# Real and imaginary parts of 64 states in one tile, two more folds of cells and one scan: one core, a gated mix of a state-space layer and linear attention

## The chip, the cores and the metric

The kernel runs on one core of one Trainium2 chip. The metric is device time in microseconds (us) of a whole execution. A core has TensorE (PE in the profile; its weight loads are PEld), VectorE (DVE), ScalarE (ACT), GpSimd (POOL) and SyncE (SP). SP, ACT and POOL also issue DMA transfers.

## The reference

Two branches read the same input x (2048 × 512) and are mixed by a gate per token. Branch A is a diagonal state-space layer with 512 complex states; branch B is linear attention with 32 heads of width 16, whose feature map is a pair of softmaxes.

```python
def _A_ref(x, ...):
    dt = exp(log_dt); Lam_bar = exp(dt * Lam)
    B_bar = ((Lam_bar - 1.0) / Lam)[:, None] * Bmat
    Bu = einsum("bld,pd->blp", x, B_bar)
    for t in range(L):
        h = Lam_bar * h + Bu[:, t, :]
    return 2.0 * einsum("blp,dp->bld", hseq, Cmat).real + x * Dskip

def _B_ref(x, wqkv, w_phi, wo):
    # q, k, v of 32 heads; pq = q @ w_phi, pk = k @ w_phi
    phi_q = concat([softmax(pq), softmax(-pq)]); phi_k = concat([softmax(pk), softmax(-pk)])
    kv = phi_k^T v; z = sum(phi_k)
    return ((phi_q kv) / (phi_q z + 1e-6)) @ wo

g = sigmoid((x * gate_w).sum(-1))
return g * a + (1 - g) * b
```

## The kernel before

**The recurrence by cells.** The 2048 time steps are 256 cells of 8; position r of a cell is the remainder r. States come in four tiles of 128 (index j), real and imaginary parts in separate planes. `b` (line 607 on) projects x on B for the even positions into `eb`; `g` projects an odd position, adds the even one before it times lambda, and goes on folding (lambda², lambda⁴), all as matmuls with diagonal matrices `dg`; a complex product of two planes is two matmuls for each plane. After three doublings `vv[j]` holds what a whole cell of 8 adds. `z` (line 658 on) runs the scan over the 256 cells on VectorE: it rotates by tabulated angles (`T2c`, `T2s`, made by `i`), scans real and imaginary parts with the real decay r⁸, and rotates back. Then the other positions of each cell are restored from the scan: `H` (position 3), `h` (1 and 5) and `p` (0, 4, 2, 6), each a complex multiple of an earlier state added to what `b` or `g` left.

In `h` and `p` this is done in two ways. For j < 2, ScalarE or VectorE scales (`scaled`, lines 434 to 438) into a scratch tile and a DMA issued by POOL adds it to its target in SBUF (`add_by_dma`, line 647). For j ≥ 2 VectorE adds.

**The output.** `y` multiplies the states of 128 tokens with C (`C2`, scaled by `c`), `o` is the attention numerator and denominator, `O` transposes its result by DMA, `t` multiplies with wo on top of `y` in the same PSUM bank and takes it out with the gate, `R` stores. Output tiles come in the order of `ORD = (7, 3, 5, 1, 0, 4, 2, 6)`, two tiles of tokens for each remainder: y0 and y1 need only the scan, y2 and y3 `H`, y4 to y7 `h`, y8 to y15 `p`.

**Branch B.** `k`, `v`, `q` are projections, their PSUM taken out to `Xq` and `vx`; `x`, `n`, `e`, `s` (`X`, `N`, `E`, `S` for Q) are maximum, minimum, exponentials and sums of the features; `a` accumulates keys times values, and in spare columns the gate's dot product, as 64 one-column matmuls. `S` ends in two DMA transposes into `phT`.

**What sets the order.** Every engine and every DMA queue runs its instructions in the order of one written list, `ORDER` (lines 24 to 52). A token is the next step of a stage: `g011@6` is a step of `g` for tile 0, second odd position, imaginary part, in PSUM bank 6; `:D` puts an eviction or scaling on VectorE in place of ScalarE. The order within one engine is the list's; across engines only data and buffers hold a step back.

Of the kernel before, what the change touches and what calls it, by code (L numbers as in the profile page):

```python
# [20 lines left out]
P = 128  # L21
# [27 lines left out]
S3 S3 y8 o10 p31 t8 o11@6 O3 t9 S3 S3 t6 o11 o11 p21 p31 t8 t9 y12@1 t7 p31:D y14@0 t6 t7 o11 o12@6 o12 p21 O5 p21
o13@2 u11 p31 y14 o12 o12 o13 y12 o13 R2 o14@6 o13 O6 o14 o14 o14 R4 u10 O7 y13@2 y13 o15@6 o15 o15 o15 t10 t10 R3 t11  # L50
t13 t11 u12 O8 u13 t12 t12 t13 u14 R5 t14 t14 R6 y15@54 y15 y15 t15 t15:D t15 R7 t15 R8 R8
# [5 lines left out]
KO = tuple(range(16))  # L57
XLOADS = ((2, 2), (4, 2), (6, 2), (8, 2), (10, 2), (12, 2), (14, 2))
# [12 lines left out]
def kernel(  # L71
# [24 lines left out]
    PT = Pst // P  # L96
    NTI = S // P
# [42 lines left out]
    vec_n = const.tile([12, P], BF16, name="vec_n")  # L140
# [5 lines left out]
    C2 = const.tile([P, 2, PT, D], BF16, name="C2")  # L146
    warm = const.tile([P, D], BF16, name="warm")
    nc.vector.memset(warm[:], 0.0)
    nc.scalar.dma_start(out=Wc[:], in_=B_w_phi.rearrange("(k hl) e f -> (hl e) k f", hl=8))
    wk_nat, xn = C2[:, 0], C2[:, 1]  # L150
# [4 lines left out]
    for n, src in enumerate((A_Lambda_im, A_Lambda_re, A_log_dt)):  # L155
        nc.gpsimd.dma_start(out=vec_n[4 * n:4 * n + 4, :], in_=src.rearrange("(j p) -> j p", p=P))
# [3 lines left out]
    Wq2 = const.tile([P, KT, DF], BF16, name="Wq2")  # L160
    maskN = const.tile([P, 4, 4], F32, name="maskN")
    eps_p = const.tile([P, 1], F32, name="eps_p")
    vec = const.tile([P, 5, KT], F32, name="vec")
    gw_b = const.tile([P, KT], BF16, name="gw_b")
# [5 lines left out]
    eb01 = const.tile([P, 2, 2, 2, N2], BF16, name="eb01")  # L170
    Dd = const.tile([P, KT, P], BF16, name="Dd")
    Drow = const.tile([P, D], BF16, name="Drow")
    NVX = 8
# [4 lines left out]
    H3 = pR.tile([P, PT, 2, ZP + N2 + 2], BF16, name="H3")  # L178
    H1 = pR.tile([P, PT, 2, N2], BF16, name="H1")
    Xq = pR.tile([P, NTI, D], BF16, name="Xq")  # L180
    nc.vector.memset(H3[:, :, :, 0:ZP], 0.0)
# [4 lines left out]
    dg = pBC.tile([P, 9, PT, P], BF16, name="dg")  # L186
    DG_NLI, DG_LR, DG_LI, DG_NMI, DG_MR, DG_MI, DG_NNI, DG_NR, DG_NI = range(9)
    (S_NLI, S_LR, S_LI, S_NMI, S_MR, S_MI, S_NNI, S_NR, S_NI, S_NBI, S_BR, S_NBR) = range(12)
    par = pBC.tile([P, 25, PT], F32, name="ssm_par")
    dgs = pBC.tile([P, 12, PT], F32, name="dgs")  # L190
    dgv = pBC.tile([P, 9, PT, 4], BF16, name="dgv")
    Bn = pBC.tile([P, PT, 2, D], BF16, name="Bn")
    CT = pBC.tile([P, PT, 2, D], BF16, name="CT")
    eb = [eb01[:, 0], eb01[:, 1], Bn[:, 0:2], Bn[:, 2:4]]
# [8 lines left out]
    BT = pAC.tile([P, 2, KT, Pst], BF16, name="BT")  # L203
    T2c = pAC.tile([P, PT, NC], BF16, name="T2c")
    T2s = pAC.tile([P, PT, NC], BF16, name="T2s")
    vv = [pAC.tile([P, 2, N2], BF16, name=f"vv{j}") for j in range(PT)]
# [20 lines left out]
    def st_Lb():  # L227
        for ri, src in enumerate((A_B_re, A_B_im)):
            for h in range(2):
                trans(out=BT[:, ri, 2 * h:2 * h + 2, :], in_=src[:, 2 * h * P:2 * (h + 1) * P])  # L230
                yield
# [6 lines left out]
    def st_Lc():  # L238
        for h in range(2):
            for ri, src in enumerate((A_C_re, A_C_im)):  # L240
                trans(out=CT[:, 2 * h:2 * h + 2, ri, :], in_=src[:, 2 * h * P:2 * (h + 1) * P])
                yield
# [22 lines left out]
    tab_g = tc.tile_pool(name="tabtmp", bufs=2, reuse_waits="tile")  # L265
    tabp = tab_g.__enter__()
    iot = tabp.tile([P, NC], F32, name="iot", bufs=1)
    identf = stg.tile([P, P], F32, name="identf", bufs=1)
    make_identity(nc, identf[:])
    nc.gpsimd.iota(iot[:], pattern=[[1, NC]], base=0, channel_multiplier=0, allow_small_or_imprecise_dtypes=True)  # L270
# [10 lines left out]
    lam, ldt, dsk = vec[:, 0:2, :], vec[:, 2, :], vec[:, 3, :]  # L281
# [6 lines left out]
    dt_, r_, om_, t0, t1, t2, den_, r2_, r4_, om8, r8_ = (par[:, 10 + k, :] for k in range(11))  # L288
# [30 lines left out]
    def st_V():  # L319
        pvt = bank([P, 12], BF16, "pvt")  # L320
        nc.tensor.transpose(pvt[:], vec_n[:], ident[0:12, 0:12])
        yield
        nc.vector.tensor_copy(out=vec[:, 0:3, :].rearrange("p n j -> p (n j)"), in_=pvt[:])
        yield

    def st_V2():
        pvt = bank([P, 8], BF16, "pvt")
        nc.tensor.transpose(pvt[:], vec_m[:], ident[0:8, 0:8])
        yield
        nc.vector.tensor_copy(out=vec[:, 3:5, :].rearrange("p n j -> p (n j)"), in_=pvt[:])  # L330
# [14 lines left out]
    def st_P():  # L345
        aexp(out=dt_, in_=ldt, func=ACT.Exp)
        yield
        VT(out=tha, in0=lam, in1=dt_.unsqueeze(1).to_broadcast([P, 2, KT]), op=ALU.mult)
# [12 lines left out]
    def st_P2():  # L361
        VS(out=om_, in0=th_, scalar1=INV_2PI, scalar2=None, op0=ALU.mult)
        yield
        VS(out=t0, in0=om_, scalar1=MAGIC, scalar2=MAGIC, op0=ALU.add, op1=ALU.subtract)
        yield
        VT(out=t1, in0=om_, in1=t0, op=ALU.subtract)
# [14 lines left out]
    def st_P4():  # L381
        VS(out=om8, in0=t0, scalar1=8.0, scalar2=None, op0=ALU.mult)
        yield
        VS(out=t2, in0=om8, scalar1=MAGIC, scalar2=MAGIC, op0=ALU.add, op1=ALU.subtract)
        yield
        VT(out=om8, in0=om8, in1=t2, op=ALU.subtract)
        yield

    def st_gw():
        nc.vector.tensor_copy(out=gw_b[:], in_=vec[:, 4, :])  # L390
        yield

    def square(out_r, out_i, b, t):
# [561 lines left out]
```

## Time and profile before

| | |
|---|---|
| runs (us) | 151.61, 151.03, 151.01; median 151.03 |
| span of the profiled execution | 149.4 us, 2839 instructions; its median of runs lies 1.6 us above it |
| TensorE busy | 142.8 us, 96% |
| VectorE busy | 139.0 us, 93% |
| ScalarE busy | 125.1 us, 84% |
| POOL busy | 26.6 us, 18% |
| DMA | 20.14 MB, mean 135 GB/s; SP's queue 53.1% of the engines' time, POOL's 18.6% |

A row of the page or of the groups by line reads: line, engine, operation, output <- input by the program's names, shape, count | busy us, mean ns of one | idle time of the engine before it and who ended it. The mean is the length of one instruction; neighbours overlap, so the pace of a series is shorter and is read from start times. A row of a stretch reads: from:to, length, then for TensorE, its weight loads, VectorE, ScalarE and POOL the busy us and the number of instructions, then the granted TensorE clock, the share of the 16 DMA engines and the GB/s that they moved. A share can stand a little over 1, since packets overlap. In slices each digit is the busy tenths of one of 40 equal parts of the span, 3.7 us each.

### The profile page before, as it was taken

What the parts mean: (1) busy time and instruction counts of PE and PEld (TensorE: products, weight loads), DVE (VectorE), ACT (ScalarE), POOL (GpSimd) and SP (SyncE); (2) the same over time, 40 slices, a digit from 0 to 9 for tenths busy, and PEclk for the clock granted to TensorE, in tenths of its full rate; (3) what the DMA queues carried; (4) which work ended last, traced back from release to release, by engine and by line L of the source; (5) the groups of instructions that cost most, each with busy time, mean ns of one, the idle gap of its engine ahead of it and who ended that gap; (6) DMA issues with size and microseconds to landing.
All of it is one profiled execution on the core that took longest, in us unless ns stands there. A gap on an engine that the chain in (4) does not pass through costs nothing.

```text
span 149.4 us, 2839 instructions
## 1 busy us (share of the span) xinstructions
PE 142.8 (96%) x1010; PEld 73.8 (49%) x1010; DVE 139.0 (93%) x338; ACT 125.1 (84%) x222; POOL 26.6 (18%) x42
## 2 busy tenths in 40 slices
PE   6999999999999999999999999999999999999980
PEld 2844444545545444464444467555444554455450
DVE  2899999999999999999999999999999999986880
ACT  3479999999999999999999999999989996552000
POOL 7403700000000341022605236011004200000000
PEclk9999999999999999999999999999999999999999
DMA  4999999991220174008274999908999996998742
GB/s 118 222 235 174 142 202 176 246 189 33 54 91 0 26 114 77 0 0 140 38 107 70 166 175 183 210 7 133 103 238 218 184 186 77 227 207 197 209 148 71
DMA packets 52959, 20.14 MB, mean 135 GB/s; under 512 B 44496, under 2 KB 52432, under 8 KB 52944
## 3 DMA queue, kind: packets, MB, share of 16 engines
q1 hardware_dynamic: 48000, 15.44, 53.1%
q0 software_dynamic: 4000, 4.20, 18.6%
q10 hardware_dynamic: 944, 0.31, 0.8%
q8 instruction: 8, 0.13, 0.4%
q14 instruction: 7, 0.06, 0.1%
HBM read 2.91 MB, written 2.10 MB: 33 GB/s over the span
## 4 chain that ended last, share of the span: by engine, by line
ACT 67%; PE 24%; issue 3%; DVE 2%
ACT EE L554 15%; PE PS L816 11%; ACT Xq L129 9%; PE PS L875 7%; ACT CT L436 6%; ACT vx L129 5%; ACT dg L436 4%; ACT H L129 3%; ACT vv L129 3%; ACT eb L129 3%; ACT Bn L129 3%; PE PS L316 2%; PE PS L835 2%; ACT lg L562 2%; ACT m L436 1%
## 5 line engine op out<-in xcount | busy, mean ns | idle before, releaser
L554 ACT ACTIVATE EE<-EE 128x2048 bf16<-128x2048 bf16 x16 | 32.5, 2066 | 0.2 <-DVE EE L548 0.2
L483 PE MATMUL PS<-WKV,xT 128*128 128x480 bf16 (+1 forms) x128 | 29.3, 373 | 0.2 <-DMA xT<-in_A_x_dram 0.2
L483 PEld LDWEIGHTS <-xT 128*128 128x128 bf16 x192 | 18.1, 98 | 19.4 <-DMA xT<-in_A_x_dram 0.7
L129 ACT CAST Xq<-PS 128x480 bf16<-128x480 f32 x32 | 20.1, 735 | 0.5 <-PE PS L483 0.5
L625 PE MATMUL PS<-xT,BT 128*128 128x512 bf16 x64 | 15.9, 379 | 0.0
L816 PE MATMUL PS<-C,H 128*128 128x512 bf16 x64 | 15.4, 378 | 0.5 <-DVE on L848 0.2
L875 PE MATMUL PS<-Wo,oT 128*128 128x512 bf16 (+2 forms) x68 | 15.5, 367 | 0.0
L613 PE MATMUL PS<-xT,BT 128*128 128x512 bf16 x64 | 15.4, 379 | 0.0
L483 PE MATMUL PS<-Wq,xT 128*128 128x480 bf16 x64 | 15.1, 366 | 0.0
L848 DVE TENSOR_TENSOR on<-PS,rd 128x512 bf16<-128x512 f32 x16 | 10.7, 681 | 2.3 <-ACT rd L842 2.3
L881 ACT ACTIVATE ot<-PS,G 128x512 bf16<-128x512 f32 (+1 forms) x8 | 4.9, 639 | 9.1 <-PE PS L875 9.1
L436 ACT ACTIVATE CT<-H,dgs 128x1024 bf16<-128x1024 bf16 x9 | 12.1, 1349 | 0.0
L129 ACT CAST vx<-PS 128x512 bf16<-128x512 f32 x16 | 11.7, 793 | 0.0
L648 POOL DMA_DIRECT2D C<-CT x4 | 5.4, 1352 | 35.0 <-ACT rc L566 31.8
L531 DVE TENSOR_TENSOR sm<-EE 128x2048 bf16<-128x2048 bf16 (+1 forms) x9 | 10.0, 1108 | 0.1
L542 DVE TENSOR_TENSOR EE<-Xq,mx 128x2048 bf16<-128x2048 bf16 (+1 forms) x9 | 10.0, 1109 | 0.0
L548 DVE TENSOR_TENSOR EE<-mn,Xq 128x2048 bf16<-128x2048 bf16 (+1 forms) x9 | 10.0, 1107 | 0.0
L613 PEld LDWEIGHTS <-BT 128*128 128x128 bf16 x64 | 6.3, 98 | 7.2 <-issue 0.2
L569 DVE TENSOR_TENSOR EE<-EE,rc 128x2048 bf16<-128x2048 bf16 x8 | 9.8, 1234 | 0.0
L625 PEld LDWEIGHTS <-BT 128*128 128x128 bf16 x64 | 6.1, 98 | 7.0
L875 PEld LDWEIGHTS <-oT 128*128 128x128 bf16 x68 | 6.1, 98 | 6.5 <-DMA oT<-on 0.5
L531 DVE TENSOR_TENSOR sm<-sm 128x512 bf16<-128x512 bf16 (+2 forms) x18 | 9.3, 516 | 0.0
(185 smaller groups left out, 325.8 us busy)
## 6 DMA issues: line engine op xcount, KB each, us to landing
out_dram<-ot SPq DMA_DIRECT2D x7, 256.0 KB, 2.4
C<-CT POOLq DMA_DIRECT2D x4, 256.0 KB, 3.9
eb<-CT POOLq DMA_DIRECT2D x4, 256.0 KB, 4.9
eb<-dg POOLq DMA_DIRECT2D x4, 256.0 KB, 5.9
WKV<-in_A_x_dram SPq DMA_DIRECT2D x3, 256.0 KB, 3.1
WKV<-in_B_wqkv_dram SPq DMA_DIRECT2D x1, 512.0 KB, 5.6
Wo<-in_B_wo_dram SPq DMA_DIRECT2D x1, 512.0 KB, 4.8
H<-CT POOLq DMA_DIRECT2D x2, 256.0 KB, 3.3
```

Source lines behind the costliest of these rows:

```text
L129: nc.scalar.copy(out=out_ap, in_=in_ap)
L436: nc.scalar.mul(out=out_ap, in_=in_ap, mul=s_)
L483: MM(out=pt[:], lhsT=xT[:, kt, ti * P:(ti + 1) * P], rhs=W[:, kt, :], start=(kt == 0), stop=(kt == KT - 1))
L531: VT(out=dst, in0=cur[:, :, :, 0:n, :], in1=cur[:, :, :, n:2 * n, :], op=op)
L542: VT(out=half(EE, 0), in0=X5, in1=live["mx", p].to_broadcast([P, L, 8, Dh, 4]), op=ALU.subtract)
L548: VT(out=half(live["EE", p], 1), in0=live["mn", p].to_broadcast([P, L, 8, Dh, 4]), in1=X5, op=ALU.subtract)
L554: aexp(out=EE[:, l_:l_ + 2], in_=EE[:, l_:l_ + 2], func=ACT.Exp)
L613: MM(out=pb[:], lhsT=BT[:, ri, kt, j * P:(j + 1) * P], rhs=cells(kt, 2 * pr), start=(kt == 0), stop=(kt == KT - 1))
L625: MM(out=pgq[:], lhsT=BT[:, ri, kt, js], rhs=cells(kt, r1), start=(kt == 0), stop=False)
L816: MM(out=py[:], lhsT=hs[j][ri], rhs=C2[:, 1 - ri, j, c:c + w], start=(j == 0 and ri == 0), stop=False)
L848: VT(out=live["on", g_][:, u], in0=pn[:, :, :, 0:Dh], in1=rd[:].unsqueeze(3).to_broadcast([P, 2, 16, Dh]), op=ALU.mult)
L875: MM(out=py[:], lhsT=oT[:, g, :], rhs=Wo[:, g, c:c + w], start=False, stop=(g == HG - 1))
```

## The change

- **The tiles.** Eight tiles m of 64 states take the place of four of 128: partitions 0 to 63 hold the real parts and 64 to 127 the imaginary parts. `LS[:, m, 0..2]` holds the positions that `eb` and `H1` held, `HH` what `H3` held. A complex product is now one matmul with a matrix of two diagonals (`dg[k, m]`: the real part on the diagonal, the imaginary part 64 off it). B is loaded plainly in this layout and then transposed from SBUF; C is scaled in the old layout and copied over by four transfers (`C`), and four adding transfers (`A`) put in the second term.
- **Two more folds.** `g` goes on within the 256 cells: pairs (lambda⁸) and fours (lambda¹⁶) by matmuls of 128 and 64 columns on strided columns, with an eviction between each. The scan is over 64 groups of four cells, all eight tiles side by side in one instruction of 512 columns, with a decay tile that is zero where a new tile begins. The swap of real and imaginary parts that the rotation needs is a matmul with `Sw`. `sa`, `sb` and `H` then unfold with matmuls and one VectorE addition out of PSUM each.
- **Restoring the other positions.** `UNITS` lists it: `hd0` to `hd3`, `ed0` to `ed3`, `dd0`, `dd1` take two tiles each by `by_dma`: scale the state, add by DMA, scale the half-swapped state, add by DMA. `dp4` to `dp7` take one tile each by `by_pe`: one matmul and one VectorE addition. The half-swapped states come from SP's transfers `XX0`, `XX1` (four) and `XX2` (two), which copy partitions 0 to 63 to 64 to 127 and back.
- **The gate** is column 481 of Q's weights; `q` has a third step that takes that column out of PSUM, and `G` runs four times for four tiles.
- **Buffers**: seven `vx` tiles for eight; `phT` alternates between `phT0` and one more buffer.
- **The list** is written anew.

```diff
+UNITS = ((1, 'hd0', 1), (1, 'hd1', 1), (1, 'hd2', 1), (1, 'hd3', 1), (0, 'ed0', 0), (0, 'ed1', 0), (0, 'ed2', 0), (0, 'ed3', 0), (2, 'dd0', 0), (2, 'dd1', 0), (2, 'dp4', 0), (2, 'dp5', 0), (2, 'dp6', 0), (2, 'dp7', 0))
...
+    def st_g(m, dst):
+        pg = bank([P, N2], F32, "pg")
+        bx(pg, m, (1, 3)[dst])
+        yield
+        MM(out=pg[:], lhsT=dg[:, 0, m, :], rhs=LS[:, m, 2 * dst], start=False, stop=(dst == 0), skip_group_check=True)
...
+        MM(out=pg[:], lhsT=dg[:, 1, m, :], rhs=LS[:, m, 1], start=False, stop=False, skip_group_check=True)
+        yield
+        evac(hc(m, 0, 1, NC, 1), pg[:, 0:NC])
+        yield
+        MM(out=pg[:, NC:N2], lhsT=dg[:, 2, m, :], rhs=hc(m, 0, 1, NC, 1), start=False, stop=False, skip_group_check=True)
+        yield
+        evac(hc(m, 0, 2, NC // 2), pg[:, NC:N2:2])
+        yield
+        MM(out=pg[:, NC + 1:N2:2], lhsT=dg[:, 3, m, :], rhs=hc(m, 0, 2, NC // 2), start=False, stop=False, skip_group_check=True)
+        yield
+        evac(hc(m, 1, 4, NC // 4), pg[:, NC + 1:N2:4])
+        yield
+        MM(out=pg[:, NC + 3:N2:4], lhsT=dg[:, 4, m, :], rhs=hc(m, 1, 4, NC // 4), start=False, stop=True, skip_group_check=True)
+        yield
+        evac(V2[:, m], pg[:, NC + 3:N2:4])
...
+    def st_X(q):
+        for h in range(2):
+            nc.sync.dma_start(out=HHs[h * HS:(h + 1) * HS, :, q * NC:(q + 1) * NC],
+                              in_=HH[(1 - h) * HS:(2 - h) * HS, :, ZP - 1 + q * (NC + 1):ZP - 1 + q * (NC + 1) + NC])
+            yield
+    def st_X2():
+        for h in range(2):
+            nc.sync.dma_start(out=HHs[h * HS:(h + 1) * HS], in_=LS[(1 - h) * HS:(2 - h) * HS, :, 1, :])
+            yield
+    def by_dma(i, u, k):
+        plain = prevs if u < 2 else (lambda m: pair(LS[:, m, 1]))
+        for part, (src, sc_) in enumerate(((plain, dgs[:, k, 0, :]), (lambda m: pair(HHs[:, m]), nsn[:, k, :]))):
+            t = slot(2 * (i % 2) + part)
+            for e in range(2):
+                m = 2 * i + e
+                scaled(pair(t[:, e]), src(m), sc_[:, m:m + 1])
+                yield
+            add_by_dma(LS[:, 2 * i:2 * i + 2, u], t)
+            yield
+    def by_pe(m, u, k):
+        pd = bank([P, N2], F32, "pd")
+        MM(out=pd[:], lhsT=dg[:, k, m, :], rhs=prevs(m) if u < 2 else LS[:, m, 1], start=True, stop=True)
+        yield
+        addto(LS[:, m, u], pd[:])
+        yield
...
-            for kt in range(KT):
-                MM(out=live["acc"][1][:, 4 * KVW + ti:4 * KVW + ti + 1], lhsT=xT[:, kt, ti * P:(ti + 1) * P],
-                   rhs=gw_b[:, kt:kt + 1], start=False, stop=(n_ == NTI - 1 and kt == KT - 1), skip_group_check=True)
...
+        VS(out=nge[:, n:n + 1], in0=pq[:, DF:DF + 1], scalar1=-Z_MAX, scalar2=-1.0, op0=ALU.max, op1=ALU.mult)
```

The new list from the scan to the last additions (in part):

```
G0 g71 g31 v11@6 g71 s3 g61 g31 g71 g51:D S0 g51 g31:D g51 q10@5 A v11 S0 z0@4 z0 v9 q10 v10@6 v12@7 v14@1 z0 z0 z0
...
H2@5 sb0 v13 q13 a4 a4 a4 H2 E1 q13 H0@4 Y H1@5 A H0 E1 Y S0 q11 q8@1 q11 H1 q8 XX0 Y H3@4 Ld H3 q9@2 Y S1 q9 q14@5
...
S1 N2 hd3 hd2 y3 G2 S1 hd3 t0 q12 S1 N3 O1 E2 q12 t1 E2 hd3:D q15 hd3:D y3 t0 y6@2 ed1 y2 t1 S1 hd2 hd2:D t3 t2 S1
hd2:D N3 X3 ed1:D hd3 t2 y5@5 S2 o4@6 o4 t3 S2 o4 S1 y7@3 S2 o5@0 Ld R0 y4@4 ed0:D hd2 ed1 o5 ed0:D o5 y4 S2 y4 o4
...
ed3:D t6 o8 y9@6 E3 o9 XX2 dd0:D dd1:D dd0 o10@0 o10 S3 o10 XX2 o10 t6 y11@7 y10@5 ed3 dd1 o11@0 S3 o11 y10 dp4@2
...
t10 G3 R2 S3 dd1 t8 dp7 o12@0 o13@3 o12 o13 u9 dp4 dd1 o13 t9 u10 R3 o12 y14@2 o12 y12@6 y14 o13 y12 t10 G3 u11
```

More of the change, by code (lines that the diff above doesn't have):

```diff
@@ L202 @@
     Wd = pAC.tile([P, HG, Dh - 1], BF16, name="Wd")
[L203 to L206, printed above, removed]
+    BT = pAC.tile([P, MT, KT, P], BF16, name="BT")
+    T2c = pAC.tile([P, MT, NC // 4], BF16, name="T2c")
+    T2s = pAC.tile([P, MT, NC // 4], BF16, name="T2s")
+    decay = pAC.tile([P, MT, NC // 4], F32, name="decay")
     stg_g = tc.tile_pool(name="stage", bufs=2)
@@ new lines, in st_A, with st_z @@
+    def st_A():
+        for q, pq_ in ((0, 0), (1, 1), (0, 1), (1, 0)):
+            add_by_dma(C2[q * HS:(q + 1) * HS, pq_::2], CT[pq_ * HS:(pq_ + 1) * HS, 1 - q])
+            yield
+    def st_z(b):
+        sw = pools["sw"][1]
+        n = MT // ZB
+        m0, m1 = b * n, (b + 1) * n
+        w_ = n * NC // 4
+        tc_, ts_ = T2c[:, m0:m1].rearrange("p m c -> p (m c)"), T2s[:, m0:m1].rearrange("p m c -> p (m c)")
+        v_ = V2[:, m0:m1].rearrange("p m c -> p (m c)")
+        pv = bank([P, w_], F32, "pz_")
+        MM(out=pv[:], lhsT=Sw[:], rhs=v_, start=True, stop=True)
+        yield
+        mc = sw.tile([P, w_], BF16, name="mc")
+        VT(out=mc[:], in0=v_, in1=tc_, op=ALU.mult)
@@ new lines, in st_H, with prevs, pair @@
+    def st_H(b):
+        pd = bank([P, 2, NC], F32, "pd")
+        for k in range(2):
+            MM(out=pd[:, k], lhsT=dg[:, 2, 2 * b + k, :], rhs=hc(2 * b + k, -1, 1, NC), start=(k == 0), stop=True, skip_group_check=True)
+        yield
+        addto(HH[:, 2 * b:2 * b + 2, ZP + NC:ZP + N2], pd[:])
+        yield
+    def prevs(m):
+        return HH[:, m, ZP - 1:ZP - 1 + 2 * (NC + 1)].rearrange("p (q c) -> p q c", c=NC + 1)[:, :, 0:NC]
+    def pair(t):
+        return t.rearrange("p (q c) -> p q c", c=NC)
@@ L841, in st_o @@
         rd = op_.tile([P, 2, 16], F32, name="rd")
[L842 removed]
+        aexp(out=rd[:], in_=ld[:], func=ACT.Exp, scale=-1.0, bias=nge[:, n:n + 1])
         yield
```

491 lines of the change are left out of this document (220 added, 271 removed).

## The prediction

> **What bounds the kernel now.** I read the page's busy line and slices first, then TensorE in order of time, then the DMA share by stretches, because the page shows three engines full at once.
>
> ```profile
> PE 142.8 (96%) x1010; PEld 73.8 (49%) x1010; DVE 139.0 (93%) x338; ACT 125.1 (84%) x222; POOL 26.6 (18%) x42
> PE   6999999999999999999999999999999999999980
> POOL 7403700000000341022605236011004200000000
> DMA  4999999991220174008274999908999996998742
> q1 hardware_dynamic: 48000, 15.44, 53.1%
> q0 software_dynamic: 4000, 4.20, 18.6%
> ```
>
> TensorE is busy in every slice but the first and the last two. "Busy" could still hide waits, so I look at the pace, in the timeline of TensorE, with VectorE's first read of the small PSUM tile and its last instruction (start, length, instruction):
>
> ```profile
> 8.63 0.17 DVE L323 CAST vec<-PS 128x12 f32<-128x12 bf16 x1
> ...
> 36.80 0.42 PE L599 MATMUL PS<-vx,EE 128*128 128x68 bf16 x8
> 37.05 0.24 PE L603 MATMUL PS<-gw_b,xT 128*128 128x1 bf16 x4
> 37.15 0.41 PE L599 MATMUL PS<-vx,EE 128*128 128x68 bf16 x8
> ...
> 38.37 0.27 PE L641 MATMUL PS<-vv,dg 128*128 128x256 bf16 x1
> 38.48 0.27 PE L642 MATMUL PS<-vv,dg 128*128 128x256 bf16 x1
> ...
> 41.33 1.89 PE L613 MATMUL PS<-xT,BT 128*128 128x512 bf16 x8
> 43.05 1.03 PE L625 MATMUL PS<-xT,BT 128*128 128x512 bf16 x4
> ...
> 92.36 1.89 PE L816 MATMUL PS<-C,H 128*128 128x512 bf16 x8
> ...
> 142.19 1.04 PE L816 MATMUL PS<-C,eb 128*128 128x384 bf16 x8
> 144.25 0.94 PE L875 MATMUL PS<-Wo,oT 128*128 128x384 bf16 x6
> 145.11 0.62 DVE L883 TENSOR_SCALAR ot<-PS,G 128x384 bf16<-128x384 f32 x1 [0.30 <-PE PS L875]
> ```
>
> Start to start, eight 512-column matmuls take 1.72 us, 0.215 each; a 256-column one 0.11; eight of 68 columns 0.25; the four gate columns 0.10. With these prices I added up TensorE's work along the ORDER list: 139.0 us in all, 88.3 ahead of y1 and 136.2 ahead of y15. The trace starts y1 at 92.36 and y15 at 142.19, so the list plus 4.1 (growing to 6.0) is the clock: TensorE stands still for hardly 2 us between them and is the bound. From the last tile's eviction at 145.1 to the end of the span it is another 4.3 us. The median of the three runs, 151.03, is 1.6 us over the profiled span of 149.4; I make the sum against the span and add 1.6.
>
> The third resource is the DMA, in stretches (the last two columns are the share of the 16 DMA engines and GB/s):
>
> ```profile
> 74.00:77.00 3.00, 3.00 (x16) 1.36 (x15) 2.92 (x9) 3.00 (x7) 0.52 (x1) 1.00 1.13 168
> 85.00:128.00 43.00, 42.17 (x375) 23.03 (x374) 42.83 (x92) 40.65 (x70) 8.17 (x7) 1.00 0.94 160
> 112.00:113.00 1.00, 1.00 (x7) 0.45 (x5) 0.97 (x6) 1.00 (x3) 0.00 (x0) 1.00 1.14 301
> 112.00:123.00 11.00, 10.68 (x81) 5.53 (x79) 10.93 (x21) 10.94 (x18) 2.43 (x2) 1.00 1.10 197
> 130.00:135.00 5.00, 5.00 (x38) 2.52 (x39) 4.25 (x9) 2.30 (x6) 0.00 (x0) 1.00 1.12 209
> ```
>
> 74 to 77 holds POOL's adding transfers alone, 130 to 135 SP's transposes alone, 112 to 123 both. The share is 1.13, 1.12 and 1.10: with both queues at work it is no higher than with one, so about 1.13 is full, and both draw on one supply. Over 85 to 128, the stretch that decides below, the share is 0.94 already. The Trainium skill, "DMA: Bandwidth & Descriptors", section "Issuing engines are not separate DMA queues", says that transfers from scalar, sync and gpsimd run on the same 16 DMA engines and interleave; the trace agrees (1.10 with both, 1.13 and 1.12 with one).
>
> **The change part by part.**
>
> *TensorE.* A turn took two matmuls per real or imaginary half, four per pair; with both halves in one tile and two diagonals it takes one per tile. Before: 48 of 512 and 16 of 256 columns, 10.3 + 1.8 = 12.1 us. After: 24 of 512, 8 of 256, and the two new folds, 8 of 128 and 8 of 64 (I take half and a quarter of 0.11), 5.2 + 0.9 + 0.4 + 0.2 = 6.7. The gate's 64 one-column matmuls go, 16 × 0.10 = 1.6; the 481st column of Q costs nothing that shows. New: two swaps for the scan, 0.43; the unfolds, 8 × 64, 8 × 128 and 8 × 256 columns, 0.2 + 0.4 + 0.9; four `dp` turns, 0.86. Sum −5.4 − 1.6 + 2.8 = −4.1 us, 134.9 in the new list. Columns of stride 2 and 4 have no row: I take no surcharge; at double price the new folds and unfolds would add 1.2. The new list's start (W11 and W10 first, the same eight warm-up matmuls) and the fewer buffers for V and `phT` I take at nothing, since the loads waited for are the same and VectorE and ScalarE get slack; ±1 us.
>
> *VectorE and ScalarE.*
>
> ```profile
> L678 DVE TENSOR_TENSOR_SCAN w<-ssm_par,mc 128x256 bf16<-128x256 f32 x8 | 5.3, 697 | 0.0
> L666 DVE TENSOR_TENSOR mc<-vv,T2c 128x512 bf16<-128x512 bf16 x4 | 1.8, 440 | 0.0
> L848 DVE TENSOR_TENSOR on<-PS,rd 128x512 bf16<-128x512 f32 x16 | 10.7, 681 | 2.3 <-ACT rd L842 2.3
> L780 DVE TENSOR_TENSOR CT<-CT,Bn 128x1024 bf16<-128x1024 bf16 x4 | 2.7, 685 | 0.0
> L129 ACT CAST vv<-PS 128x256 bf16<-128x256 f32 x16 | 9.1, 668 | 0.0
> L436 ACT ACTIVATE CT<-H,dgs 128x1024 bf16<-128x1024 bf16 x9 | 12.1, 1349 | 0.0
> L436 ACT ACTIVATE dg<-H,dgs 128x512 bf16<-128x512 bf16 x7 | 5.9, 865 | 0.0
> ```
>
> and two pieces of the chain that ended last, which give ScalarE's pace (start, us):
>
> ```profile
> 48.54 1.05 ACT CT L436
> ...
> 76.13 0.61 ACT mc L436
> ```
>
> The scan stage was 40 VectorE instructions, some 17 us by rows like L666 and L678; one scan of 512 with six products and sums is about 4.5 (512-wide 0.44, out of PSUM 0.68 by L848, scan twice 0.66). The rest nearly cancels: unfolding, 7 additions out of PSUM, 4.8, for 5.5; `dp`, 4 × 0.68, for the additions of tiles 2 and 3 in `h` and `p` (9 us by rows like L780); 16 gate columns at up to 0.17 (L323), 2.7 at most; some 15 evictions moved over from ScalarE, 5. In all VectorE does about 9 us less. ScalarE loses 14 to 16: 35 scalings of 29 us become 29 of about 18 (1024 wide 1.05, 512 wide 0.61 in the chain), the sine tables shrink from 8 calls to 2, and the five moved whole evictions go; the 16 V evictions become 32 smaller ones, +1 for their number. They form a chain ahead of the one scan: four hops of a matmul (0.38 long) and an eviction (0.67 at most), each covered by a V or Q tile of 0.86; what stays open is 0.2 a hop, 1 us, inside the ±1. Neither was ahead of TensorE, so these buy nothing; they only give slack. POOL gets the squares, the decay tile and two products for the new folds, a few us, in the first half where POOL's slices are at 0. Loading B plainly and then transposing it from SBUF, and C's four copies, lie before 85 us, where the DMA slices of 40 to 80 us stand between 0 and 8.
>
> So far the span would be 149.4 − 4.1 = 145.3.
>
> *The DMA.* This part I hold to decide. So far the state update outside TensorE went by adding DMAs for half of the states (j < 2): 12 in `h` and `p`, spread from 66 to 115 us (POOL in order of time):
>
> ```profile
> 66.17 0.89 POOL L648 DMA_DIRECT2D H<-CT  x1 [9.44 <-ACT CT L436]
> ...
> 114.27 2.43 POOL L648 DMA_DIRECT2D eb<-dg  x2 [12.75 <-ACT dg L436]
> ```
>
> Now `hd0`–`hd3`, `ed0`–`ed3`, `dd0` and `dd1` have two each, 20 adding DMAs of 256 KB, and since there is one scan for all states none can start before it. New besides are the half swaps: `XX0`/`XX1`, 4 × 256 KB, and `XX2`, 2 × 512 KB. In the new list the first swap stands behind 83.1 us of TensorE work, at 83.1 + 4.1 = 87 us; `y14`, whose first matmul reads what `dd0` and `dd1` add, at 123.8, so at 128 to 130. Between them must pass: 20 × 0.262 = 5.2 MB of adding, A's last 0.26, swaps 2.1, `phT` transposes 6 × 0.524 = 3.1, `oT` 6 × 0.262 = 1.6, outputs and x 0.8: 13.1 MB in 41 to 43 us, 305 to 320 GB/s. Before, 160 GB/s × 43 = 6.9 MB passed there with the share at 0.94. That doesn't fit. At the rates of the full stretches: adding 5.5 MB at 168 GB/s, 32.7 us; transposes 4.7 at 209, 22.6; plain copies 2.9 at about 290 (the 301 row, and less), 10. Sum 65.3, so `y14` starts at 87.2 + 65.3 = 152.5 in place of 129. After it TensorE has 134.9 − 123.8 = 11.1 us and the end 4.3: span 167.9, and with 1.6 a time of **169.5**. Bounds: everything at 168 GB/s is 78 us and 182; at the best single microsecond, 301, it is 43.6 and 148, where the overload vanishes. I take the mix, since adding is the largest part and its own row is the lowest.
>
> While this backlog stands, the wait sits on compute queues too: the scalings of `hd2` write the buffer that `hd0`'s DMA reads, so ScalarE and VectorE wait there with exponentials and evictions behind them; SP waits at `XX2` for all of `hd`, with `oT`, `phT` and output transfers behind. That can only lengthen it.
>
> **The rivals.**
>
> A, *the transfers fit* (faster). If the 16 engines move the mix at over about 320 GB/s, the DMA never sets the end and TensorE's 4.1 us are the gain: 145.3 + 1.6 = 147.0. For it: 301 GB/s stands in one row, and the list keeps TensorE supplied with V and Q tiles around the scan. Against it: that microsecond lies behind an output store, a plain copy, and no stretch with adding transfers passes 197. The Trainium skill, same page, section "Anatomy of one DMA", fits a DMA as 2.0 us plus bytes / 436e3; by it the 13.1 MB would be an estimated 30 us of movement, and the time A's. The trace differs, with 168 to 209 GB/s at full share.
>
> B, *late, not full*. Two additions into one tile go one behind the other, and the list leaves little TensorE work between the second and its reader: 3.0 us at `y6`, 0.9 at `y4`, 0.3 at `y10`, none at `y14`.
>
> ```profile
> eb<-CT POOLq DMA_DIRECT2D x4, 256.0 KB, 4.9
> eb<-dg POOLq DMA_DIRECT2D x4, 256.0 KB, 5.9
> H<-CT POOLq DMA_DIRECT2D x2, 256.0 KB, 3.3
> ```
>
> At 4.9 us from issue to landing the four places cost 1.9 + 4.0 + 4.6 + 4.9 = 15.4 at most, 4.9 at least: 147.0 + 5 to 15, say 156 (152 to 162). It speaks for B that the share counts packets in flight, and for my forecast that packets of both queues together never raised it.
>
> C, *A and B cancel*: stalls of 4 us eat the gain, no change.
>
> **How the numbers follow.** Full DMA 0.62 (own range 158 to 184), B 0.18, A 0.15, C 0.05. The time is that of the first. 151 to 184 leaves out A, C and little more. What a measurement here can tell from no change is about 0.5%, 0.8 us: faster is A, 0.15; same C, 0.05; slower 0.80.
>
> **What would show it.** Right: the DMA slices at 9 from about slice 22 nearly to the end; TensorE with gaps that begin between y6 and y8 and are longest before y14, with waits of matmuls, or of the scalings, for DMAs into `LS`; q0 near 28% × 149.4 us of 16 engines' time; adding DMAs landing in well over 6 us; VectorE and ScalarE with some 9 and 15 us less work. TensorE's busy sum is no test of its work, since pipelined ends are modelled. Wrong: TensorE unbroken with span near 145 (A), or gaps with the DMA share under 0.9 there (B). The size fails if the full rate for adding isn't 168 GB/s, or if the engines are held up by their own waits so long that the DMA runs empty.

## The result, and the profile after

The changed kernel takes 189.31 us (median of 4 runs, 188.5 to 190.99) against 151.03 for the kernel before (151.01 to 151.61). The ratio is 1.252, with a 95% interval of 1.246 to 1.259. The forecast was 169.5, in a range of 151 to 184: slower was right, the size was not. The profiled execution has a span of 187.2 us, 2.1 below the median of the runs. A median here is of all runs of a kernel, a ratio of those within 1.5% of its fastest.

The page after, engines, slices, queues and the chain that ended last:

```profile
PE 151.1 (81%) x944; PEld 76.1 (41%) x960; DVE 141.5 (76%) x323; ACT 114.4 (61%) x216; POOL 48.6 (26%) x72
PE   6499994978999999999898995918099717696992
...
DVE  2466999999999999999997997545536707667791
...
PEclk9859998799999999999999999696859995799999
DMA  6999989800160177921927699999999999999952
...
q1 hardware_dynamic: 53312, 19.63, 58.3%
q0 software_dynamic: 6688, 6.30, 25.1%
...
DMA 35%; DVE 30%; PE 20%; ACT 7%; issue 5%; POOL 1%; POOLq 0%; DVEq 0%; ACTq 0%
```

Counted from 0, VectorE is full from slice 4 and TensorE from slice 10, both up to slice 23. In the slices ahead VectorE shows 2 to 6 tenths, where the kernel before has 8 and 9 from slice 1 on. From slice 23 the DMA is full, TensorE has holes, its clock falls in them, and the chain that ended last, which is DMA to 35%, runs through the transfers. The same in order of time (start, length, engine, line), with the first projection (L516), the first product of keys and values (the KV product, L633), the first half swap (SPq, L774), the first adding transfers (POOL, L684) and TensorE's longer stops:

```profile
8.36 0.17 PE L341 MATMUL PS<-ident,vec_n 24*128 24x24 bf16 x1 [2.35 <-DMA vec_n<-in_A_log_dt_dram]
...
11.32 1.01 PE L516 MATMUL PS<-WKV,xT 128*128 128x480 bf16 x2
...
31.22 3.08 PE L516 MATMUL PS<-WKV,xT 128*128 128x480 bf16 x8 [2.35 <-DVE Xq L137]
...
32.26 4.35 POOL L458 TENSOR_TENSOR dg<-I,dgv 128x1024 bf16<-128x1024 bf16 x2
...
32.82 2.02 DVE L566 TENSOR_TENSOR mx<-mx 128x512 bf16<-128x512 bf16 x1
...
34.76 1.93 DVE L566 TENSOR_TENSOR mn<-mn 128x128 bf16<-128x128 bf16 x1
...
40.46 0.42 DVE L566 TENSOR_TENSOR mn<-mn 128x512 bf16<-128x512 bf16 x1
...
48.51 0.68 PE L633 MATMUL PS<-vx,EE 128*128 128x68 bf16 x16
...
98.04 0.61 SPq L774 DMA_DIRECT2D CS<-HH  x1
...
105.54 2.44 POOL L684 DMA_DIRECT2D LS<-CT  x2 [31.24 <-ACT ld L870]
...
117.11 1.89 PE L848 MATMUL PS<-C,LS 128*128 128x512 bf16 x4 [2.30 <-DMA LS<-CT]
121.47 1.03 PE L848 MATMUL PS<-C,LS 128*128 128x512 bf16 x4
126.93 0.52 PE L866 MATMUL PS<-KVm,phT 128*128 128x68 bf16 x8 [4.43 <-DMA phT<-EE]
...
135.98 1.89 PE L848 MATMUL PS<-C,LS 128*128 128x512 bf16 x4 [4.99 <-DMA LS<-CT]
...
155.24 0.63 PE L866 MATMUL PS<-KVm,phT 128*128 128x68 bf16 x8 [4.60 <-DMA phT<-EE]
...
171.19 0.59 PE L848 MATMUL PS<-C,LS 128*128 128x512 bf16 x2
172.31 3.20 PE L848 MATMUL PS<-C,LS 128*128 128x512 bf16 x14 [0.54 <-DMA LS<-CT]
```

The first swap starts at 98.0, where the forecast had 87.2. `y14` has all that `dd0` and `dd1` add at 172.3 (the last line; two of its matmuls, which read tiles 0 and 1, ran at 171.2), where the forecast had 152.5; from there to the end it is 14.9 us, where it had 15.4. So 10.8 us are missing ahead of the first swap and 9.0 between it and `y14`. The stretches (PE, PEld, DVE, ACT and POOL busy, then clock, DMA share and GB/s), after:

```profile
0.00:20.00 20.00, 15.62 (x83) 8.11 (x85) 10.54 (x53) 10.27 (x20) 6.40 (x19) 0.83 0.98 194
20.00:100.00 80.00, 74.58 (x482) 38.22 (x489) 78.19 (x164) 65.03 (x115) 18.15 (x33) 0.98 0.54 94
...
98.00:172.00 74.00, 51.88 (x331) 25.35 (x333) 45.19 (x97) 39.60 (x79) 24.06 (x20) 0.86 1.16 174
120.00:130.00 10.00, 5.57 (x32) 2.60 (x32) 4.25 (x8) 3.17 (x8) 4.01 (x4) 0.84 1.34 125
```

and before:

```profile
0.00:20.00 20.00, 18.52 (x105) 9.55 (x106) 16.23 (x82) 14.59 (x31) 8.48 (x26) 1.00 0.98 178
20.00:100.00 80.00, 79.80 (x578) 41.17 (x577) 79.92 (x180) 79.99 (x134) 14.52 (x13) 1.00 0.58 105
```

174 GB/s over 74 us are 12.9 MB, nearly the 13.1 of the forecast. What the forecast did not read is VectorE: it too was full from 20 to 100 us before (79.92 of 80), and is after (78.19); but after, it has done only 10.54 us of its work by 20 us, and before it had done 16.23. It begins with the list's start: the first projection of the kernel before, 3.4 us earlier than after's at 11.32, is

```profile
7.91 0.58 PE L483 MATMUL PS<-WKV,xT 128*128 128x480 bf16 x2
```

### The profile page after: what moved, and what is told of

Read it like the earlier page. It is cut to its first block, busy times and chain, and to the rows that moved or that the text cites. A ratio compares the mean times of both kernels' runs of the same rounds, so it can differ in the third digit from the quotient of the medians.

```text
span 187.2 us, 2800 instructions
## 1 busy us (share of the span) xinstructions
PE 151.1 (81%) x944; PEld 76.1 (41%) x960; DVE 141.5 (76%) x323; ACT 114.4 (61%) x216; POOL 48.6 (26%) x72
## 3 DMA queue, kind: packets, MB, share of 16 engines
q0 software_dynamic: 6688, 6.30, 25.1%
## 4 chain that ended last, share of the span: by engine, by line
DMA 35%; DVE 30%; PE 20%; ACT 7%; issue 5%; POOL 1%; POOLq 0%; DVEq 0%; ACTq 0%
DMA LS<-CT 25%; DMA phT<-EE 7%; PE PS L516 5%; DVE mx L566 5%; DVE mn L566 4%; DVE EE L577 4%; PE PS L643 4%; DVE EE L583 3%; PE PS L848 3%; ACT EE L589 3%; DVE sm L566 3%; DMA vec_n<-in_A_log_dt_dram 3%; PE PS L648 2%; DVE EE L604 2%; DVE HH L738 1%
## 5 line engine op out<-in xcount | busy, mean ns | idle before, releaser
L684 POOL DMA_DIRECT2D LS<-CT x20 | 24.1, 1350 | 68.9 <-ACT ld L870 33.4
L848 PE MATMUL PS<-C,LS 128*128 128x512 bf16 (+1 forms) x101 | 29.4, 428 | 10.2 <-DMA LS<-CT 9.7
L516 PE MATMUL PS<-WKV,xT 128*128 128x480 bf16 (+1 forms) x122 | 31.0, 397 | 3.4 <-DVE Xq L137 2.3
L516 PEld LDWEIGHTS <-xT 128*128 128x128 bf16 x192 | 18.8, 101 | 24.2 <-issue 7.7
L135 ACT CAST Xq<-PS 128x480 bf16<-128x480 f32 x31 | 16.6, 572 | 4.8 <-PE PS L516 4.8
L848 PEld LDWEIGHTS <-LS 128*128 128x128 bf16 x104 | 10.2, 110 | 22.7 <-DMA LS<-CT 12.0
L879 DVE TENSOR_TENSOR on<-PS,rd 128x512 bf16<-128x512 f32 x16 | 10.7, 687 | 10.9 <-ACT rd L873 10.9
L904 PE MATMUL PS<-Wo,oT 128*128 128x512 bf16 (+2 forms) x66 | 15.4, 376 | 0.9 <-DMA oT<-on 0.9
L516 PE MATMUL PS<-Wq,xT 128*128 128x481 bf16 x64 | 15.4, 366 | 0.9 <-DVE HH L738 0.9
L866 PE MATMUL PS<-KVm,phT 128*128 128x68 bf16 x128 | 7.5, 213 | 10.5 <-DMA phT<-EE 10.3
L135 ACT CAST LS<-PS 128x512 bf16<-128x512 f32 x23 | 13.3, 596 | 1.5 <-PE PS L648 1.3
L684 POOL DMA_DIRECT2D C<-CT x4 | 4.2, 1576 | 33.5 <-DMA C<-CS 33.5
L866 PEld LDWEIGHTS <-phT 128*128 128x128 bf16 x128 | 6.5, 110 | 14.7 <-DMA phT<-EE 12.2
L135 ACT CAST vx<-PS 128x512 bf16<-128x512 f32 x14 | 8.0, 600 | 4.2 <-PE PS L516 4.2
L566 DVE TENSOR_TENSOR mn<-mn 128x256 bf16<-128x256 bf16 (+3 forms) x27 | 10.0, 372 | 0.3
```

The lines of the kernel that those rows point to most:

```text
L135: nc.scalar.copy(out=out_ap, in_=in_ap)
L516: MM(out=pt[:], lhsT=xT[:, kt, ti * P:(ti + 1) * P], rhs=W[:, kt, 0:pt.shape[-1]], start=(kt == 0), stop=(kt == KT - 1))
L566: VT(out=dst, in0=cur[:, :, :, 0:n, :], in1=cur[:, :, :, n:2 * n, :], op=op)
L684: nc.gpsimd.dma_start(out=out_ap, in_=in_ap, accum_op=ALU.add)
L848: MM(out=py[:], lhsT=hs[m], rhs=C2[:, m, c:c + w], start=(m == 0), stop=False)
L866: MM(out=pn[:, hf, 4 * m:4 * m + 4, :].rearrange("p h e -> p (h e)"), lhsT=ph[:, 4 * hf + m, :], rhs=KVm[:, 4 * hf + m, :], start=(m == 0) ...
```

## The experiments

Theory T1, the forecast's: the bytes of the 20 adding transfers and the half swaps fill the DMA engines from the first swap to `y14`. Rival T2: not the bytes but the order of the transfers, which wait for each other's landings, slots and queues. Rival T3: neither; the one scan, its folds and unfolds and the new list cost the time. For the 10.8 us at the front, theory F: VectorE's work ahead of the first swap sets it. Single runs have no interval; the changed kernel's own runs spread over 2.5 us. Where the list ahead of the swap is untouched (the change, e2, e3, e7, e8), the first swap stands at 96.3 to 98.5 and the first KV product at 46.7 to 49.2, so a shift of less than some 2 us says nothing there.

**e3: no adding transfers.**

```diff
-            add_by_dma(LS[:, 2 * i:2 * i + 2, u], t)
```

> Edit: the 20 adding transfers are left out, and with them all that they add to LS; scalings and half swaps stay. T1: the 7.7 MB that are left take 33 us at the rates of their rows (209 and 290 GB/s), the stretch from the first swap to y14 is 41 us of TensorE's list, so the DMA is no bound: 145.3 + 11 lost before + 2 = 158 (156 to 163). T2: the same 158. T3 (scan, folds, list): 180 or more. Against e2 it says how much of the price is in the bytes: if e2 saves about half of what e3 saves, bytes; if e2 saves almost nothing, the number and order of the transfers.

Measured 160.05 us, 29.3 less than with them and inside T1's range. Its page:

```profile
PE 141.4 (89%) x944; PEld 73.6 (46%) x960; DVE 140.6 (89%) x323; ACT 113.8 (72%) x216; POOL 24.5 (15%) x52
...
PEclk9999999999999999999999999999999999999999
...
q0 software_dynamic: 1248, 1.06, 6.0%
```

T3 falls as the main cause: three quarters of the 38.3 us go with the transfers. The same 944 matmuls are 141.4 us here and 151.1 with the transfers, and the clock row is all 9: the holes also made TensorE slow. But 160.05 is 13 us above the 147.0 of the forecast's rival A. The first swap stands at 96.9 here, so 9.7 of the 13 lie ahead of it, and 3.4 behind it (158.4 − 96.9 = 61.5 us against A's 145.3 − 87.2 = 58.1). The granted clock of the first 20 us is 1.00 here and 0.83 in the change, whose swap is only 1.1 us later: the clock is not what made the front late.

**e2: half of each adding transfer.**

```diff
-            add_by_dma(LS[:, 2 * i:2 * i + 2, u], t)
+            add_by_dma(LS[:, 2 * i, u], t[:, 0])
```

> Edit: each of the 20 adding transfers carries only the even tile of its pair, 128 KB for 256 KB; their number, their places, their waits, the scalings and the half swaps stay. Left out of the computation: what the transfers add to the odd tiles of LS. T1 (bytes): 2.6 MB less at the 168 to 174 GB/s of the full stretches is 15 us: 174 (171 to 178). T2 (the number of transfers and their waits for each other): 185 to 189. T3: 189.

Measured 170.97, 18.3 less, just below T1's range and far from T2's. With number, order and waits as they were, half the bytes are worth 62% of the whole: bytes, as T1 says.

**e7: the same transfers, copying and not adding.**

```diff
-            add_by_dma(LS[:, 2 * i:2 * i + 2, u], t)
+            nc.gpsimd.dma_start(out=LS[:, 2 * i:2 * i + 2, u], in_=t)
```

> Edit: the 20 transfers into LS are plain copies of the same 256 KB on the same queue, in the same places and with the same waits; only the addition at the target is gone. Left out of the computation: what was in LS before them is overwritten. Theory T1 with the row of 168 GB/s for adding (a byte that is added costs more than a byte that is copied): 5.2 MB at about 290 take 18 us for 31, so 176 (172 to 180), and q0 falls from 47 us of 16 engines to under 35. Rival (copying from SBUF to SBUF costs that much with or without the addition, or bytes don't count): 186 to 191, q0 as before.

Measured 177.41, 11.9 less for the same bytes. From the page and the list of transfers:

```profile
q0 software_dynamic: 2848, 6.30, 14.8%
...
LS<-CT POOLq DMA_DIRECT2D x20, 256.0 KB, 4.6
```

q0 took 26.0 us of 16 engines (14.8% of 175.7), with the addition 47.0 (25.1% of 187.2), without the transfers 9.5. So adding 5.24 MB costs the engines 37.5 us in 5440 packets (6688 less 1248), and copying it 16.5 us in 1600. In the engines' time the addition costs 2.3 times the copy.

Since the front varies from run to run, the stretch from the first swap to `y14` compares these runs better than their totals:

| | first swap | `y14` | between | MB between |
|---|---|---|---|---|
| the change | 98.0 | 172.3 | 74.3 | 12.89 |
| e7, copies | 98.5 | 159.1 | 60.6 | 12.95 |
| e2, half added | 96.3 | 154.3 | 58.1 | 10.41 |
| e3, none | 96.9 | 143.4 | 46.5 | 7.63 |

The adding transfers are worth 27.8 us there, their second half 16.2, and the addition alone 13.7. The first half is worth less because without any the engines are no longer full: the DMA share between is 0.84 in e3 and 1.17 in the change. What e2 and e7 don't separate is rate and landing: with less to move a transfer also lands sooner (4.8 and 4.6 us for 6.8), and what waits for a landing waits less.

**e8: seven slots for four.**

```diff
-            t = slot(2 * (i % 2) + part)
+            t = slot(seq[0] % 7)
+            seq[0] += 1
```

> Edit: the scalings have seven buffers in turn for four; the three new ones lie in the V tiles, which are free by then. A scaling waits for the landing of the seventh transfer before it and no longer for the fourth. T1 (the engines are full, a buffer more only lets the queue grow): 186 to 190, no change beyond 1%, the landings of the adding transfers longer than 6.8 us. Rival T2 (waits for slots hold ScalarE and VectorE, 12.1 + 6.5 us, and with them the exponentials and evictions behind): minus 6 to 12 us, 177 to 183.

Measured 190.11, ratio to before 1.251 (1.241 to 1.260), the changed kernel's own; T2's 177 to 183 falls. The waits for slots that T2 counted, in the changed kernel's list of waits (us in all, times, longest),

```profile
DVE CT L467 <- DMA LS<-CT: 12.1, 5, 5.7
...
ACT CT L465 <- DMA LS<-CT: 6.5, 4, 2.4
```

are gone in e8's list of waits and nothing is won: they are where the full DMA shows, not what costs.

**e1: all units over TensorE.** Every `hd`, `ed` and `dd` pair becomes two tiles by `by_pe`, and the half swaps go.

```diff
-UNITS = ((1, 'hd0', 1), (1, 'hd1', 1), ... (2, 'dp6', 0), (2, 'dp7', 0))
+UNITS = ((1, 'hp0', 1), (1, 'hp1', 1), ... (2, 'dp6', 0), (2, 'dp7', 0))
```

> Edit: the units hd, ed and dd (20 adding transfers, their 40 scalings) become 20 tiles hp, ep, dp of the form of dp4 to dp7 (one matmul on TensorE, one addition on VectorE); the half swaps XX0, XX1, XX2 go. 7.3 MB leave the DMA engines. Theory T1 (the DMA engines are full from the first half swap to y14, bytes decide): nothing of that stretch is full any more, so the span is TensorE's list, 134.9 + 20 x 0.215 = 139.2, plus 4.1 of the old lag, 11 lost before the first swap, 4.3 of end, 158.6, and 2.1 to the median: 161 (157 to 167, the upper end if VectorE's 20 more additions of 0.69 us make it late). Rival T2 (not the bytes but the order: each transfer waits for another's landing): the same, since the transfers go with their waits. Rival T3 (neither: the one scan, the chain of folds and unfolds and the new list cost the time): 180 or more.

Measured 175.65, ratio 1.158 (1.152 to 1.165): better than the change, 15 us worse than T1 said and outside its range. The groups:

```profile
L862 PE MATMUL PS<-C,LS 128*128 128x512 bf16 (+1 forms) x100 | 24.0, 371 | 4.0 <-DVE LS L752 3.8
...
L752 DVE TENSOR_TENSOR LS<-PS,LS 128x512 bf16<-128x512 f32 x24 | 16.1, 685 | 5.5 <-PE PS L813 5.2
```

The 24 additions are 16.1 us of VectorE, and the two engines wait for each other, 3.8 and 5.2 us. With this list neither DMA nor VectorE has room for the work. Those waits don't add up to the 15 us, and whether a better order would win them back was not tried.

**e5: less VectorE work ahead of the swap.**

```diff
-                VT(out=E5[:, u:u + 2], in0=E5[:, u:u + 2], in1=rc[:, u:u + 2]...
```

> Edit: the eight VectorE multiplications by rc (1.218 us each, from 44.1 to 86.5 us) are left out, 9.7 us of VectorE work that all lies ahead of the first half swap. Left out of the computation: the normalisation of the key features. Theory F (VectorE, busy 76.5 of 78.0 us from 20 us to the first swap at 98.0, sets the first swap): the first swap comes 7 to 9.5 us earlier, at 89 to 91, where TensorE's list becomes the limit, and the time falls with it: 181 (179 to 184). Rival G (TensorE's own list, loads and clock set it): first swap at 96 to 98, time 188 to 190.

Measured 191.29, the first swap at 96.9: nothing won, and **e6**, the same on top of e3, took 162.36 for e3's 160.05, with the first swap at 98.0.

> Edit: e5 and e3 together: neither the eight multiplications nor the 20 adding transfers. Left out of the computation: both. If the two causes are separate and add up, T1 and F: 160.05 less 7 to 9.5, 151.5 (150 to 154), and TensorE is unbroken from 20 us on, so that the change without its two costs would be where before is. Rival (VectorE's work is the limit only because something else is late too, or the tail has a bound of its own): 157 or more.

F falls as I had put it. All the work that e5 took away lay behind 44 us. From 48 to 96 us VectorE is busy for 38.4 us in e5 (47.1 in the change) and TensorE for 47.4 (47.1): TensorE hasn't a stop to give back there; it was late by then already.

**e4 and e9: the front.** `V` moves behind the second fold of Wk, `Db` goes from GpSimd to VectorE; e9 has its last product earlier besides.

```diff
-... W00 V@1 Lx W01 T0@5 Lx T0 T1@3 f0@6 W10:D f0 T1 f1@4 f1:D V ...
+... W00 Lx W01 T0@5 Lx T0 T1@3 f0@6 W10:D f0 T1 f1@4 V@1 f1:D V ...
...
-        TT, TC = (VT, nc.vector.tensor_copy) if k0 == 0 else (GT, nc.gpsimd.tensor_copy)
+        TT, TC = VT, nc.vector.tensor_copy
```

> Edit: V (the transpose of vec_n) moves in the list from ahead of the x transposes to behind the second fold of Wk, and Db (two turn matrices) goes from GpSimd to VectorE. TensorE's stop of 2.35 us at 8.36 and VectorE's two instructions at 32.8 and 34.8 that took 3.95 for 0.64 us beside GpSimd's go. Theory E1 (what is lost before the first swap is passed on whole, as the backlog begins when the first swap does): minus 3 to 3.4 for V, minus 1 to 2 for Db (3.3 less the two products of 0.70 us that VectorE now does), 184.5 (182.5 to 186). Rival E2 (the lost time is in the clock and in loads, not in these two places): 188 to 190.

e4 took 188.48, ratio 1.245 (1.237 to 1.254): not told apart from the change. Its first KV product came 5.3 us earlier, but TensorE then waited for `Db`'s last product, and the first swap came at 95.4:

```profile
66.91 0.23 PE L693 MATMUL PS<-HH,dg 128*128 128x64 bf16 x1 [2.94 <-DVE dg L473]
```

> Edit: e4, and the third Db token (the turn matrix that TensorE waited for at 66.9 us in e4) stands some 100 places earlier in the list. Theory F2, in place of F (VectorE holds TensorE only up to 48 us; from there TensorE goes unbroken, and what it has lost by then it keeps): e4's first KV product came at 43.2 for 48.5, and without the stop of 2.94 the first half swap comes at 92 to 93.5 for 98.0; the backlog behind it starts as much earlier: 185 (183 to 187.5). Rival H (VectorE is full all the way, and what is won early is lost again before the scan): first swap at 95 or later, 187 to 190.

e9 took 186.53, ratio 1.223 (1.219 to 1.228), where the change has 1.252 (1.246 to 1.259). Its four runs are 184.54, 190.52, 185.4 and 187.66; two of them lie in or next to the change's 188.5 to 190.99, so the gain in time is less sure than the swap's. Its first stretch, and its first KV product and first swap in order of time:

```profile
0.00:20.00 20.00, 16.57 (x99) 8.24 (x101) 13.65 (x65) 12.61 (x25) 8.25 (x23) 1.00 0.95 198
```

```profile
43.42 0.67 PE L648 MATMUL PS<-vx,EE 128*128 128x68 bf16 x16
...
93.12 0.61 SPq L789 DMA_DIRECT2D CS<-HH  x1
```

The swap is 4.9 us earlier, and with the same front it stands at 94.0 in e10 and 92.8 in e11, all ahead of the 96.3 to 98.5 of the untouched front. VectorE has 3.1 us more done by 20 us (13.65 for 10.54), and 1.9 fewer to do after it (the two products of 0.70 in place of the 3.3 us lost beside GpSimd, rows at 32.8 and 34.8): 5.0. From the first swap to `y14` it is 74.8 us, as in the change: what is won ahead is passed on.

**e10 and e12: the front without the full DMA.** e10 is e9 with e3. e12 is e3 with three of four levels of the first trees left out:

```diff
+            if key in SHORT and n < Dh // 2:
+                live[key] = cur = cur[:, :, :, 0:n, :]
...
+                continue
```

> Edit: e9 and e3 together; left out of the computation: what the 20 transfers add to LS. It reads e9's gain without the full DMA behind it. F2: e3's 160.05 less the 3.5 to 5 us by which the first swap is earlier than its 96.9: 156 (155 to 157). H: 158.5 to 160.5.

> Edit: e3, and in the trees of maxima and minima of the first three key groups only the first of four levels is done, 18 VectorE instructions less, 4 to 4.5 us, all ahead of 42 us. Left out of the computation: the other three levels (a maximum over fewer features), and what the 20 transfers add to LS. Theory F2 (VectorE holds TensorE up to 48 us, and TensorE keeps what it lost): against e3 the first KV product comes 3 to 4.5 us earlier (43 to 44.4 for 47.4) and so does the first half swap (92.5 to 94 for 96.9), 156 to 157.5 for e3's 160.05; e5 took away twice as much VectorE work, but behind 44 us, and won nothing. Rival (what holds TensorE early is loads and ScalarE): first KV product at 46.5 or later, 159 to 161.

e10 took 158.41 (first swap 94.0), e12 158.94 (94.1; first KV product 44.6), e3 160.05 (96.9; 47.4). In e12, from the timelines of its TensorE and SP's queue:

```profile
44.60 0.68 PE L655 MATMUL PS<-vx,EE 128*128 128x68 bf16 x16
...
94.13 0.61 SPq L796 DMA_DIRECT2D CS<-HH  x1
```

So VectorE work taken away ahead of 42 us moves the swap: of some 4 us in e12, 2.8 show, in an execution whose first tree starts 1.1 us later than e3's (16.8 for 15.7). Both swaps lie ahead of the 96.3 of the untouched front, but both moved less than F2 said, and both times miss its ranges (e10's is next to H's): of the 2.8 and 2.9 us only 1.1 and 1.6 reach the end, in single runs. F2 holds for the swap in direction; behind it part is lost again, and why is not shown.

**e11: a mix.** e9, with `hd` and `dd` by `by_pe` and only `ed` by DMA, in `hd`'s places.

> Edit: e9, and in the tail hd and dd go over TensorE and VectorE (twelve tiles hp and dp, as in e1), ed stays with its eight adding transfers and takes hd's places in the list; XX2 goes. 4.2 MB less than before for the DMA engines, 8.9 MB from the first swap to y14, at 174 to 200 GB/s 45 to 51 us for a list of 43: nearly fits. T1 and F2: TensorE's 134.9 + 12 x 0.215 = 137.5, lag 10, end 4.3, and some waits: 157 (153 to 162), better than e1's 175.65 and after's 189.31, not better than before's 151. Rival V (what cost e1 15 us over e3 is VectorE, whose additions TensorE waits for, and 12 of the 20 are still there): 164 to 172.

Measured 174.57 (171.24 to 178.88): far worse than T1 and F2 said, and for the most part above V's 172, though it has eight adding transfers and twelve additions where e1 has twenty. One stretch of it:

```profile
120.00:130.00 10.00, 5.31 (x45) 2.73 (x45) 6.72 (x14) 3.00 (x10) 0.13 (x1) 0.90 1.25 184
```

The eight transfers, bunched now, still fill the engines there. In the whole tail TensorE waits 4.6 us for `phT` and 4.7 for the additions, so both kinds of wait are in it. Why it is no better than e1's stays open.

## Why the prediction was right and wrong

**Right: what the adding transfers cost.** The forecast had 31.2 us for 5.2 MB at 168 GB/s, 15.6 for half of them and 13.1 for the addition alone (31.2 less 18.1 as copies). Between the first swap and `y14` they are worth 27.8, half of them 16.2, and the addition 13.7. The signs were as listed: DMA slices at 9 from slice 23 to near the end, landings of 6.8 us, waits of matmuls and scalings for `LS`.

**Wrong, the larger part: "the new list's start ... I take at nothing ... ±1 us" and "Neither was ahead of TensorE, so these buy nothing; they only give slack".** The first swap was 10.8 us late. The loss was early: up to 48 us TensorE was busy for 39.2 us, in the kernel before for 46.5, so about 7 of the 10.8 were gone by then (about 8 of 9.7 in e3). VectorE was 5.7 us behind by 20 us (16.23 less 10.54; other executions of the untouched front had done 11.5 to 12.7), and lost 3.3 beside GpSimd's `Db`, and TensorE stopped for its evictions (the row at 31.22). What the runs show of this is some 4 us: e9, which touched only these two, got back 4.9 against the change, its front in e10 2.9 against e3, and e12's cut on VectorE alone 2.8. The other 6 or so are not shown; of the 5.7 us by 20 us e9 still lacks 2.6. I had read TensorE as the bound because it was full; from 20 us on VectorE was as full, so that its late work became TensorE's late work. e5 shows the limit of that: behind 48 us the same cut buys nothing.

**Wrong, the smaller part: 200 GB/s for the mix** (13.1 MB in 65.3 us). It was 174, 9.0 us more. The step that failed is the sum of rates that were read in stretches with one kind of transfer, not the rate for adding: by the same rates the stretch would take 52.2 us with copies and 49.7 with half added, and it took 60.6 and 58.1. The excess, 9.0, 8.4 and 8.4, is nearly the same in the three. Some 2 us of it come before the first adding transfer: from 98.0 to 105.5 us the DMA share was 0.66 and 145 GB/s passed, where the forecast had the engines full from the first swap on. Where the rest lies stays open; the six `phT` transposes between took 10.3 us each to land (median), 7.1 in e7, 6.4 in e2 and 4.8 in e3. And "about 1.13 is full" was no limit: the share reached 1.34 while 125 GB/s passed. The sentence that the compute queues' waits "can only lengthen it" was right in sign and had no number; TensorE's matmuls alone were 9.7 us longer than in e3, at the lower clock.

**Smaller points.** VectorE's instructions add up to 160.7 us by their lengths, for 166.2 before: 5.5 less where I said 9, while its busy time rose from 139.0 to 141.5, since they overlap by 19.2 us in all and before by 27.2. ScalarE lost 10.7, not 14 to 16. q0 took 47.0 us of the engines, not 41.8. TensorE's longest stop was not before `y14` (4.99 us at 136.0, before `y14` 0.54), and two of the four over 2 us behind the swap waited for `phT`, whose transposes shared the engines with the additions.

**The rivals.** A fell twice: the transfers didn't fit, and without them the time is 160, not 147. B (late, not full) fell by its own sign, the DMA share of 1.16 where it wanted under 0.9, and by its size; in e8 the waits for slots are gone and nothing is won, while e2 and e7 leave open how much of the price is paid as later landings. C fell with the result. No version here is faster than the kernel before.

## What to carry to other kernels

When two engines are full, a change that relieves one can be lost if the other starts its work later: compare each engine's work done by an early point (here 20 and 48 us), not only its total. Price a transfer by its kind (an adding one cost about twice a copy here, 27.8 us for 14.1 over 20 of them), sum the bytes that must pass between two fixed points of the list, and take the rate from a stretch with the same mix; the sum of single rates was 8.4 to 9.0 us short in three mixes here. A late transfer can cost TensorE twice, the stop and the half pace behind it.

## What the runs showed of the hardware

- The addition makes a transfer dear: 272 packets for 256 KB and 1.9 us of all 16 engines, against 80 packets and 0.8 for the plain copy (e7, e3).
- VectorE instructions of two SBUF inputs took 2.02 and 1.93 us while GpSimd multiplied `dg`; the 512-wide one takes 0.42 alone (rows at 32.8, 34.8 and 40.5). The Trainium skill, "SBUF — State Buffer", section "Who interferes with whom", says that a VectorE instruction with two SBUF inputs contends with a GpSimd instruction that reads SBUF; the trace agrees.
- Four 512-column matmuls took 1.89 us behind stops of 2.30 and 4.99 us, 1.03 otherwise; the granted clock was 0.50 from 117 to 118 us, behind the first. The Trainium skill, "TensorE: Matmul & The Clock Gate", section "HAM oscillation — how this bites in real kernels", puts a return to half clock behind idle gaps over about 3.4 us; here four matmuls behind a stop of 2.30 us were as slow. The length of one stop doesn't decide it alone: behind 2.35 us at 31.22 the change's eight matmuls took 3.08 us, and behind the same stop in e3 1.78:

```profile
30.10 1.78 PE L531 MATMUL PS<-WKV,xT 128*128 128x480 bf16 x8 [2.35 <-DVE Xq L152]
```
